# A fifth group of five turned by DMA ahead of the last rows, and x held until earlier transfers have landed

## The chip, the core and the metric

The kernel runs on one core of a Trainium2 chip. A core has TensorE (matmuls; PE in the profile, its weight loads PEld), VectorE (DVE), ScalarE (ACT), GpSimd (POOL) and SyncE (SP), each with its own instruction stream, and 16 DMA engines that all streams share. SP and GpSimd issue this kernel's transfers: SP's make up the queue "hardware_dynamic" of the profile, GpSimd's "software_dynamic". Matmuls write to PSUM banks; VectorE and ScalarE empty them to SBUF. The metric is the device time of one execution in microseconds (us), the median of several.

## What is computed

A mix along the sequence in the frequency domain, and then a mixer with a low-rank part and a hidden layer, for 8 batches of 3136 positions with 256 channels:

```python
X = np.fft.rfft(x, axis=1)                  # x: 8 x 3136 x 256
y = np.fft.irfft(X * F, n=3136, axis=1)     # F = filt_r + 1j * filt_i
h = y.transpose(0, 2, 1) @ U @ V            # rank 32
u = y + h.transpose(0, 2, 1)
out = u + np.maximum(u @ w_ch1, 0) @ w_ch2  # 256 -> 1024 -> 256
```

Inputs and output are float32; the matmuls take float16.

## The kernel before

**Stages of one batch.** The transform of length 3136 is split as 49 x 64. Stage 1 (`f1`) multiplies x by a matrix of the 49-point transform and stores the result in DRAM (`ct1`, `ct0`, L256 and L257). Batches 2 to 7 load it back turned as the tiles `a2`: four loads on SP, issued at once (L330 and L327, the first 512 KB ahead of a 32 KB and two more of 512 KB). Batches 0 and 1 turn it on TensorE instead. Stage 3 (`mid`) does the 64-point transform (`pz`, L385), the product with the filter on VectorE (`uv`, L393 to L398) and the way back (`pe`, L344), and stores its result in DRAM (`ct2`, L363) in three parts. `load_e2` loads the parts back as rows of the tile `eb` (L417), each in two halves; a part can be loaded when its last store has landed. `rank` computes the low-rank part and spreads it over 32 more rows of `eb` (L439). Stage 4 (`s4`, L457) multiplies `eb` by a constant matrix and gives u, transposed, in the tile `ut` (two buffers).

**Groups.** The mixer works through the 25088 positions in 49 groups of 512. Group n has eight steps `mm1` (L489, hidden layer, ReLU on ScalarE at L492), and, one group later, eight steps `mm2` (L522) that add into a PSUM bank `pc` (two banks). A slot is one step of both: slot 8n+t runs `mm1` of group n and `mm2` of group n-1. After steps 3 and 7 of `mm2` half a group is moved by VectorE from `pc` to `och` (two buffers, used in turn by the groups), and after step 7 GpSimd stores the group (L542).

**The u in `u + ...`.** The output is not transposed and `ut` is. Either TensorE adds u: eight matmuls with `ut` as weights and the identity as moving data (`residual`, L514), and VectorE copies the sum (L538). Or the group's stretch of `ut` is turned by two DMA transposes on SP (`turn_u`, L502, one for each half of the channels) into the tile `tur` (three buffers), and VectorE adds it while it empties `pc` (L535). 35 of the 49 groups are in the set `turning`. Of the six groups that begin in each batch's stretch, the first straddles two batches; for batches 2 to 6 of the loop, groups 10, 16, 22, 28 and 34 are the fifth, and are added by TensorE, like these first ones.

**What sets the order.** The program is scheduled by hand: each engine runs its instructions in the order in which the program issues them. The list `plan` has, for each of the 392 slots, generators that are advanced by a step after that slot's `mm1` and `mm2`. In the loop at L618, batch b's stages 3 and 4 lie in the slots from `a = S[b-1]` to `z = S[b]` (for b = 2: 48 to 96), in which the mixer works on the batch before; `e = z - 20` (22 from b = 6 on) is where stage 3 ends. The last part of the rows is loaded at `e + 1`, a2 of batch b+1 at `e + 2`, `s4` begins at `e + 8`. The four loads of x for batch b+1 are dealt to slots a-8, a-6, a-4 and a-2 (L640). GpSimd's stream from there on has only output stores and loads of x; those loads wait for stage 1 of the batch before, which is through by then.

Of the kernel before, what the change touches and what calls it, by code (L numbers as in the profile page):

```python
# [14 lines left out]
NB = 8  # L15
# [14 lines left out]
def row_of(k1, part):  # L30

    return 4 * (2 * ((k1 - 1) % 8) + part) + (k1 - 1) // 8
# [47 lines left out]
def kernel(  # L80
# [11 lines left out]
    nc = tc.nc  # L92
# [22 lines left out]
    def dram(t, off, dims):  # L115
        return bass.AP(tensor=t, offset=off, ap=[list(d) for d in dims])
# [7 lines left out]
    def load_x(b, c):  # L124
        t = sb.tile([98, 8 * DM], F16, tag="x", bufs=4, name="x")
        for a, n in ((0, 96), (96, 2)) if b == 0 else ((0, 98),):
            nc.gpsimd.dma_start(t[a:a + n], dram(x.tensor, (b * SEQ + 8 * c + 32 * a) * DM, [[32 * DM, n], [1, 8 * DM]]))
        xt[b, c] = t
# [68 lines left out]
    seen = cst.tile([128, 4], F16)  # L197
# [95 lines left out]
    def turn(b, g):  # L293
        if g == 3:
            t = a20[b]
            pt = bank("z" if b else "o", "pt", F16)
            for dh in range(2):
                nc.tensor.transpose(pt[0:64, 128 * dh:128 * dh + 128], t1[b][1][:, dh, :], idn)
            nc.scalar.copy(t[0:64], pt[0:64, 0:DM])
            return t  # L300
        t = sb.tile([128, 8, DM], F16, tag="a2", bufs=3, name="a2")
        for half in range(2):
            pt = bank("m" if b == 0 and g == 1 and half == 0 else "z", "pt", F16)
            if b == g == half == 0:
                unread(pt.bitcast(F32), 2)
            for i in range(4):
                for dh in range(2):
                    nc.tensor.transpose(pt[:, 256 * i + 128 * dh:256 * i + 128 * dh + 128],
                                        t1[b][0][:, dh, 8 * g + 4 * half + i, :], idn)
            (nc.scalar.copy if half or (g and b == 0) else nc.vector.tensor_copy)(  # L310
                t[:, 4 * half:4 * half + 4, :].rearrange("p k d -> p (k d)"), pt)
        return t
# [2 lines left out]
    PAIRS = [(k, k + 1) for k in range(1, NK, 2)]  # L315
    e3 = {}

    def mid(b, tag="z"):
        a2 = {}

        def load_a2(g):
            if b < 2:
                a2[g] = turn(b, g)
                return
            if g == 3:
                t = a20[b % 2]
                nc.sync.dma_start(t[0:64], ct0[b].ap())  # L327
            else:
                t = sb.tile([128, 8, DM], F16, tag="a2", bufs=3, name="a2")
                nc.sync.dma_start(t, dram(ct1[b], 8 * g * DM, [[24 * DM, 128], [1, 8 * DM]]))  # L330
            a2[g] = t

        def s3(ks, uv, o):
            n = len(ks) * DM
            i = (ks[0] - 1) // 2
            pe = bank(tag, "pe")

            direct = b == 0 and ks[0] > 22
            ms = (gmp, gsmp) if direct or not ks[0] else (gm, gsm)
            if b == 0 and ks[0] > 8:  # L340

                unread(pe, 1)
            for f, w in enumerate(ms if b == 0 else ms[:1]):
                nc.tensor.matmul(pe[:, 0:n], w, uv[:, f, o:o + n], start=(f == 0), stop=(b > 0 or f == 1))  # L344
            if not ks[0]:
                e3[b, 6] = sb.tile([128, DM], F16, tag="e30", bufs=1, name="e30")
                nc.scalar.copy(e3[b, 6], pe[:, 0:n])

                nc.sync.dma_start(eb[96:97, :, :], e3[b, 6][0:64])
                return  # L350
            if i % 2 == 0:
                e3[b, i // 2] = sb.tile([128, 4, DM], F16, tag="e3", bufs=6, name="e3")
            t = e3[b, i // 2]
            nc.scalar.copy(t[:, 2 * (i % 2):2 * (i % 2) + 2, :].rearrange("p k d -> p (k d)"), pe)  # L354
            if direct:
                for n, k in enumerate(ks):
                    for part in range(2):
                        (nc.sync if part else nc.gpsimd).dma_start(
                            eb[32 + row_of(k, part):33 + row_of(k, part), :, :],
                            t[64 * part:64 * part + 64, 2 * (i % 2) + n, :])  # L360
            elif i % 2 or b == 0 and i == 10:
                n = 4 if i % 2 else 2
                nc.sync.dma_start(dram(ct2[b][i // 4], 2 * (i % 4 // 2 * 2) * 128 * DM, [[DM, 128], [128 * DM, n], [1, DM]]), t[:, 0:n, :])  # L363

        if b == 0:
            spread_filters(0)
        for g in (0, 3, 1, 2) if b > 1 else (0, 3):
            load_a2(g)
        if b > 1:
            yield  # L370
        todo = []
        first_at = 2 if b < 2 else 6
        for i, ks in enumerate(PAIRS[:first_at] + [(0,)] + PAIRS[first_at:]):
            n = len(ks) * DM
            if b == 0 and i == 1:
                spread_filters(1)
            if b < 2 and i in (3, 7):
                load_a2(i // 4 + 1)
            pz = bank("z", "pz")
            if b == i == 0:  # L380
                unread(pz, 2)
            if ks[0]:
                src = a2[(ks[0] - 1) // 8]
                k = (ks[0] - 1) % 8
                nc.tensor.matmul(pz, a2m, src[:, k:k + 2, :].rearrange("p k d -> p (k d)"), start=True, stop=True)  # L385
            else:
                nc.tensor.matmul(pz[:, 0:n], a20m, a2[3], start=True, stop=True)
            o = 512 if ks[0] % 4 == 3 else 0
            if o == 0:
                uv = sb.tile([128, 2, 1024], F16, tag="uv", bufs=4, name="uv")  # L390
            zin = bass.AP(tensor=pz.tensor, offset=pz.offset, ap=[[pz.ap[0][0], 128], [0, 2], [1, n]])
            fin = view(fab[:, 0, ks[0], 0:1], 0, [[NK * DM, 2], [1, n]])
            nc.vector.tensor_mul(uv[:, :, o:o + n], zin, fin)  # L393
            todo.append((ks, uv, o))
            if b and (o or not ks[0]):

                nc.vector.tensor_sub(uv[0:64, 0, 0:o + n], uv[0:64, 0, 0:o + n], uv[64:128, 1, 0:o + n])  # L397
                nc.vector.tensor_add(uv[64:128, 0, 0:o + n], uv[64:128, 0, 0:o + n], uv[0:64, 1, 0:o + n])  # L398
            if len(todo) > (3 if b else 2):
                s3(*todo.pop(0))  # L400
            yield
        for n, it in enumerate(todo):
            s3(*it)
            if b or n == 0:
                yield
        if b == 0:
            load_e2(0, 2, [0])
            for part in range(3):
                load_e2(0, part, [1])
        yield  # L410
# [71 lines left out]
    def utv(b):  # L482
        return ut[b].rearrange("p h q r -> p h (q r)")
# [14 lines left out]
    def turn_u(gr):  # L498
        gr.tu = sb.tile([128, 2, 4, 128], F16, tag="tur", bufs=3, name="tur")
        for b, t0, o, n in gr.seg:  # L500
            for dh in range(2):
                nc.sync.dma_start(gr.tu[:, dh, :, :], utv(b)[:, dh, t0:t0 + n], transpose=True)  # L502
        yield

    def residual(gr, o, i):
# [42 lines left out]
    def deal(gen, count, a, z):  # L548
        for i in range(count):
            plan[max(0, int(a + i * (z - a) / count))].append(gen)  # L550

    def later_x(b, c):
        load_x(b, c)
        yield

    def turn_at(at, n):
        turning.add(n)
        plan[at].append(turns[n])
# [59 lines left out]
    for b in range(1, NB):  # L618
        a, z = S[b - 1], S[b]
        e = z - (17 if b == 1 else 20 if b < 6 else 22)  # L620
        deal(mids[b], 13, a + {1: 8, 2: -3}.get(b, -5), e - 4)
        deal(mids[b], 4, e - 4, e)
        for p, at in enumerate((e - 5, e - 4, e + 1)):
            plan[at].append(loads(b, p))
        deal(ranks[b], 6, e, e + 6)
        if b + 1 < NB:

            plan[z - 12 if b == 1 else e + 2].append(mids[b + 1])

        n = a // 8 + (1 if b > 1 else 2)  # L630
        for i in range(3):
            turn_at(a + (15 if b == 1 else 1) + i, n + i)
        turn_at(z - (15 if b == 1 else 9), z // 8 - 1)
        deal(s4s[b], 16, e + 8, z - 2)
        if b == 1:
            deal(f1s[1], 12, 1, 8)
        if b + 1 < NB:

            for c in range(4):
                plan[a + (9 if b == 1 else -8) + 2 * c].append(later_x(b + 1, c))  # L640
            deal(f1s[b + 1], 16, a + (21 if b == 1 else 10), z - (13 if b == 1 else 20))
# [43 lines left out]
```

## Time and profile before

| | before |
|---|---|
| median of 3 runs, us | 509.52 |
| the three runs, us | 506.11, 509.73, 509.52 |
| profiled execution, us | 511.49 |
| its span (first to last instruction), us | 509.7 |
| mean granted TensorE clock | 0.989 |
| residual matmuls (L514) | 120, busy 15.5 us |
| transposes (L502) | 70, 1.35 us median to issue one on SP |
| moved by SP's queue, by GpSimd's | 55.06 MB, 41.58 MB |

Durations come from the profiled execution. "Busy" of TensorE counts a matmul from its start to the modelled end of its pipeline, so that neighbours overlap; what a matmul costs is read from the starts. The granted clock is 1.00 or 0.50 of full speed, and the half-clock stretches before the end last 3.41 and 6.83 us. The page's 40 slices (12.7 us each) show where TensorE, its clock and the DMA engines fall off:

```profile
PE   4887899969999999999999999999999999999996
PEclk9998999998999999999999999999999999999999
DMA  8988769997568985899578995899688447443233
```

The costliest groups on TensorE, ScalarE and VectorE (busy us, mean ns of one, idle before it and what ended that):

```profile
L492 ACT ACTIVATE h<-phh 128x512 f16<-128x512 f32 x392 | 236.1, 605 | 87.4 <-PE phh L489 86.6
L522 PE MATMUL pc<-w2sb,h 128*128 128x256 f16 x1568 | 234.8, 273 | 1.3 <-DMA w2sb<-in_moe_w_ch_dram 0.8
L489 PE MATMUL phh<-ut,w1sb 128*128 128x512 f16 (+7 forms) x896 | 234.5, 354 | 0.4 <-DVE ut L464 0.4
...
L393 DVE TENSOR_TENSOR uv<-pz,fab 128x1024 f16<-128x1024 f32 (+1 forms) x104 | 120.6, 1178 | 15.0 <-PE pz L385 13.5
L535 DVE TENSOR_TENSOR och<-pc,tur 128x512 f32<-128x512 f32 (+1 forms) x71 | 48.4, 682 | 77.7 <-PE pc L522 76.5
```

### The profile page before, as it was taken

Reading aid. Unit: us, or ns where it says so; the run is one execution under the profiler, and the core shown is the slowest. Engines: PE = TensorE matmul, PEld = TensorE weight load, DVE = VectorE, ACT = ScalarE, POOL = GpSimd, SP = SyncE. Lnnn points to the kernel's source line nnn. Section 1 sums busy time; section 2 is a strip of 40 time slices with the busy share of each in tenths; the row PEclk is TensorE's granted clock in tenths of the full one; section 3 lists DMA queues with packets and bytes.
Section 4 is the critical chain, followed back from the end, with each engine's and each line's share of the span. In section 5 each row is a group of like instructions: output and inputs, shape, how many; then the busy total and the mean of one; then the engine's idle time right before and its main releaser. Section 6 shows DMA issues by size and latency. Waiting matters only on the chain.

```text
span 509.7 us, 11525 instructions
## 1 busy us (share of the span) xinstructions
PE 483.3 (95%) x4572; PEld 339.6 (67%) x4572; DVE 351.5 (69%) x470; ACT 375.3 (74%) x704; POOL 80.4 (16%) x123
## 2 busy tenths in 40 slices
PE   4887899969999999999999999999999999999996
PEld 4536566756666777677667777677677766776664
DVE  5887699457866898479757887579847896732122
ACT  6865779945896689867896689767996677666662
POOL 6662110020100200120101101021001010101110
PEclk9998999998999999999999999999999999999999
DMA  8988769997568985899578995899688447443233
GB/s 195 164 211 193 115 143 232 256 232 189 159 191 274 235 201 158 253 284 195 162 228 287 195 197 156 263 262 179 208 247 246 125 115 228 125 125 105 80 107 125
DMA packets 105471, 97.39 MB, mean 191 GB/s; under 512 B 42931, under 2 KB 89971, under 8 KB 105416
## 3 DMA queue, kind: packets, MB, share of 16 engines
q1 hardware_dynamic: 90712, 55.06, 43.3%
q0 software_dynamic: 14704, 41.58, 31.2%
q8 instruction: 36, 0.59, 0.5%
q14 instruction: 19, 0.16, 0.1%
HBM read 55.20 MB, written 47.78 MB: 202 GB/s over the span
## 4 chain that ended last, share of the span: by engine, by line
PE 79%; DMA 9%; DVE 5%; ACT 2%; issue 0%; POOL 0%; ACTq 0%; SPq 0%
PE pc L522 30%; PE phh L489 29%; PE pu L457 5%; PE pf L249 4%; PE pe L344 4%; PE pz L385 4%; DVE uv L393 3%; DMA ct<-e 3%; DMA eb<-ct 2%; DMA w2sb<-in_moe_w_ch_dram 2%; DMA a<-ct 2%; PE pc L514 1%; PE ph L424 1%; ACT e L354 1%; ACT h L492 1%; ACT asb L254 1%
## 5 line engine op out<-in xcount | busy, mean ns | idle before, releaser
L492 ACT ACTIVATE h<-phh 128x512 f16<-128x512 f32 x392 | 236.1, 605 | 87.4 <-PE phh L489 86.6
L522 PE MATMUL pc<-w2sb,h 128*128 128x256 f16 x1568 | 234.8, 273 | 1.3 <-DMA w2sb<-in_moe_w_ch_dram 0.8
L489 PE MATMUL phh<-ut,w1sb 128*128 128x512 f16 (+7 forms) x896 | 234.5, 354 | 0.4 <-DVE ut L464 0.4
L522 PEld LDWEIGHTS <-h 128*128 128x128 f16 x1568 | 151.9, 98 | 93.2 <-issue 3.1
L393 DVE TENSOR_TENSOR uv<-pz,fab 128x1024 f16<-128x1024 f32 (+1 forms) x104 | 120.6, 1178 | 15.0 <-PE pz L385 13.5
L535 DVE TENSOR_TENSOR och<-pc,tur 128x512 f32<-128x512 f32 (+1 forms) x71 | 48.4, 682 | 77.7 <-PE pc L522 76.5
L542 POOL DMA_DIRECT2D out_dram<-och x48 | 38.8, 809 | 392.8 <-DVE och L535 265.4
L489 PEld LDWEIGHTS <-w1sb 128*128 128x128 f16 x896 | 80.2, 98 | 21.0 <-issue 2.1
L354 ACT CAST e<-pe 128x512 f16<-128x512 f32 x96 | 56.6, 591 | 16.4 <-PE pe L344 15.5
L464 DVE CAST ut<-pu 128x392 f16<-128x392 f32 x92 | 48.8, 560 | 18.5 <-PE pu L457 16.9
L254 ACT CAST asb<-pf 98x512 f16<-98x512 f32 x96 | 57.2, 599 | 0.1
L439 DVE COPY eb<-h 32x4096 f16<-32x4096 f16 x32 | 38.2, 1231 | 13.8 <-ACT h L436 13.8
L457 PE MATMUL pu<-sv,eb 97*128 97x49 f16 x1024 | 40.5, 187 | 3.4 <-DMA eb<-ct 3.4
L344 PE MATMUL pe<-uv,m 128*128 128x512 f16 (+1 forms) x117 | 41.3, 371 | 2.5 <-DVE uv L393 2.4
L457 PEld LDWEIGHTS <-eb 97*128 97x128 f16 x1024 | 38.2, 98 | 5.6 <-DVE eb L439 2.8
L385 PE MATMUL pz<-a,m 128*128 128x512 f16 x96 | 36.7, 384 | 5.3 <-DMA a<-ct 4.3
L249 PE MATMUL pf<-x,ws 98*98 98x256 f16 x192 | 36.7, 273 | 0.1
L397 DVE TENSOR_TENSOR uv<-uv 64x1024 f16<-64x1024 f16 (+1 forms) x49 | 30.9, 630 | 1.7
L398 DVE TENSOR_TENSOR uv<-uv 64x1024 f16<-64x1024 f16 (+1 forms) x49 | 30.7, 627 | 0.7
L538 DVE COPY och<-pc 128x512 f32<-128x512 f32 x28 | 19.4, 691 | 15.1 <-PE pc L514 14.6
L249 PEld LDWEIGHTS <-ws 98*98 98x98 f16 x192 | 22.8, 125 | 9.5 <-issue 0.8
L462 ACT CAST ut<-pu 128x392 f16<-128x392 f32 x36 | 17.5, 485 | 8.1 <-POOL seen L605 4.0
(80 smaller groups left out, 235.7 us busy)
## 6 DMA issues: line engine op xcount, KB each, us to landing
out_dram<-och POOLq DMA_DIRECT2D x48, 512.0 KB, 4.5
ct<-e SPq DMA_DIRECT2D x47, 256.0 KB
eb<-ct SPq DMA_DIRECT2D x46, 256.0 KB
x<-in_x_dram POOLq DMA_DIRECT2D x28, 392.0 KB, 8.4
ct<-asb SPq DMA_DIRECT2D x24, 384.0 KB
a<-ct SPq DMA_DIRECT2D x18, 512.0 KB
x<-in_x_dram POOLq DMA_DIRECT2D x4, 384.0 KB, 8.0
tur<-ut SPq DMA_TRANSPOSE x70
```

The source lines that it names most:

```text
L249: nc.tensor.matmul(pf[0:98, 256 * s:256 * s + 256], ws[:, (8 * c + j) * 98:(8 * c + j + 1) * 98], t[:, j, :], start=(s == 0), stop=True, s ...
L254: nc.scalar.copy(dst, src)
L344: nc.tensor.matmul(pe[:, 0:n], w, uv[:, f, o:o + n], start=(f == 0), stop=(b > 0 or f == 1))
L354: nc.scalar.copy(t[:, 2 * (i % 2):2 * (i % 2) + 2, :].rearrange("p k d -> p (k d)"), pe)
L385: nc.tensor.matmul(pz, a2m, src[:, k:k + 2, :].rearrange("p k d -> p (k d)"), start=True, stop=True)
L393: nc.vector.tensor_mul(uv[:, :, o:o + n], zin, fin)
L457: nc.tensor.matmul(pu[:, NQ * i:NQ * i + NQ], eb[:, 8 * n + i, d], sv[:, 8 * g + i, :], start=(i == 0), stop=True, skip_group_check=True)
L464: nc.vector.tensor_copy(dst, src)
L489: nc.tensor.matmul(ph[:, o:o + n], w1sb[:, dh, 128 * t:128 * t + 128], utv(b)[:, dh, t0:t0 + n], start=(dh == 0), stop=(dh == 1), skip_gro ...
L492: nc.scalar.activation(h, ph, RELU)
L522: nc.tensor.matmul(o, gr.h[tt][:, 128 * i:128 * i + 128], w2sb[:, tt, :], start=(tt == 0), stop=(tt == 7 and gr.n in turning), skip_group_ ...
L535: nc.vector.tensor_add(dst.rearrange("p g (h d) -> p g h d", h=2), src.rearrange("p (g h d) -> p g h d", h=2, d=128), gr.tu[:, :, a:a + n, ...
```

## The change

1. For batches 2 to 6, the fifth group of the stretch (10, 16, 22, 28 and 34) joins the set `turning`. Its two transposes are issued in slot `e`: on SP after stage 3's last store and stage 1's last store of those slots, and ahead of the last part of the rows.
2. The third turned group of a stretch (9, 15, 21, 27, 33 and 39) is issued in slot a+8 in place of a+3. By then a buffer of `tur` is free.
3. `last_in[b]` holds a piece of the last tile that SP was told to fill for batch b: the last tile of a2 for batch 2, and the turned stretch of group 11, 17, 23 or 29 for batches 3 to 6. For batches 3 to 7 GpSimd copies four elements a partition of it into the tile `seen` before the first load of x. So GpSimd, whose stream is in order, issues x of batch 3 once a2 of batch 2 has landed, and x of batches 4 to 7 once that group's transposes have landed.

```diff
@@ mid(), load_a2
                 nc.sync.dma_start(t, dram(ct1[b], 8 * g * DM, [[24 * DM, 128], [1, 8 * DM]]))
+                if g == 2:
+                    last_in[b] = t[:, 7, 0:4]
@@ turn_u(gr)
                 nc.sync.dma_start(gr.tu[:, dh, :, :], utv(b)[:, dh, t0:t0 + n], transpose=True)
+        if gr.n % 6 == 5:
+            last_in[gr.n // 6 + 2] = gr.tu[:, 1, 3, 0:4]
@@ later_x(b, c)
+        if c == 0 and b > 2:
+            nc.gpsimd.tensor_copy(seen, last_in[b - 1])
         load_x(b, c)
@@ for b in range(1, NB)
         deal(ranks[b], 6, e, e + 6)
+        if 1 < b < NB - 1:
+            turn_at(e, z // 8 - 2)
...
         for i in range(3):
-            turn_at(a + (15 if b == 1 else 1) + i, n + i)
+            turn_at(a + (15 + i if b == 1 else (1, 2, 8)[i]), n + i)
```

More of the change, by code (lines that the diff above doesn't have):

```diff
@@ L316 @@
     e3 = {}
+    last_in = {}
     def mid(b, tag="z"):
```

## The prediction

> **What bounds the kernel.** I read the page first (busy shares, the chain that ended last), then the waits of TensorE alone, then the chain piece by piece around each of TensorE's waits. Batches count from 0; a slot is one pair of steps `mm1`/`mm2`, eight to a group, and slot 8n+t is step t of group n.
>
> ```profile
> PE 483.3 (95%) x4572; PEld 339.6 (67%) x4572; DVE 351.5 (69%) x470; ACT 375.3 (74%) x704; POOL 80.4 (16%) x123
> ...
> PE 79%; DMA 9%; DVE 5%; ACT 2%; issue 0%; POOL 0%; ACTq 0%; SPq 0%
> ```
>
> And TensorE's waits (us in total, times, longest):
>
> ```profile
> PE pz L385 <- DMA a<-ct: 4.3, 1, 4.3
> PE pu L457 <- DMA eb<-ct: 3.4, 3, 2.5
> ```
>
> TensorE is the bound: every instruction taken off it counts, and every wait put before it counts. After the first 60 us it has three waits worth a line: one of 4.27 us for a2 of batch 2, and 0.24 and 0.62 us (batches 2 and 5) of the 3.4 for the last rows of `eb`. The first, by the chain and by windows (columns: stretch, its length, busy time of PE, PEld, DVE, ACT, POOL, granted clock, DMA share, GB/s):
>
> ```profile
> 105.78 8.83 DMA a<-ct
> 114.61 0.05 issue
> 114.66 0.61 PE pz L385
> ```
>
> ```profile
> 110.40:114.60 4.20, 0.00 (x0) 0.00 (x0) 0.39 (x1) 0.48 (x1) 0.00 (x0) 0.74 1.25 271
> 114.70:119.20 4.50, 4.50 (x17) 2.25 (x18) 1.71 (x2) 1.19 (x2) 0.00 (x0) 0.50 0.99 266
> 119.30:124.00 4.70, 4.70 (x41) 3.27 (x40) 4.62 (x7) 2.96 (x6) 0.79 (x1) 1.00 1.10 252
> ```
>
> The reader is to see that TensorE does nothing for 4.2 us, and then runs at half clock until 119.27. What a2 competes with is in GpSimd's timeline: the four loads of x for batch 3 are issued just ahead of a2.
>
> ```profile
> 102.88 0.75 POOL L542 DMA_DIRECT2D out_dram<-och  x1 [8.17 <-DVE och L535]
> 103.62 2.18 POOL L127 DMA_DIRECT2D x<-in_x_dram  x4
> 119.70 0.79 POOL L542 DMA_DIRECT2D out_dram<-och  x1 [13.90 <-DVE och L535]
> ```
>
> Second, the chain into stage 4 of batch 2: the last store of stage 3, its landing, the last rows, TensorE. It is tight in every batch: s4 starts 0.05 to 0.25 us after these rows' first half has landed.
>
> ```profile
> 152.86 5.63 DMA ct<-e
> 158.49 0.02 issue
> 158.51 3.38 DMA eb<-ct
> 161.89 0.05 issue
> 161.94 0.59 PE pu L457 x16
> ```
>
> Landings of SP's transfers below are read from the trace's semaphore events (16 steps a transfer), those of GpSimd's from its issues.
>
> **Residual matmuls removed.** Groups 10, 16, 22, 28 and 34 lose 8 matmuls of L514 each, 40 in all. The row's 220 ns is the time through the pipeline; what a pair costs is where the next matmul starts:
>
> ```profile
> 167.96 0.28 PE L514 MATMUL pc<-idn,ut 128*128 128x128 f16 x2
> ...
> 168.07 0.58 PE L457 MATMUL pu<-sv,eb 97*128 97x49 f16 x16
> ```
>
> 0.11 us a pair, so 20 x 0.11 = **2.2 us less**, all on the path. VectorE's addition (L535, 682 ns) replaces a copy (L538, 691 ns): nothing.
>
> **x of batch 3 waits for a2 of batch 2.** This takes x off the DMA engines while a2 moves. Lost before: 4.27 us idle, and 114.66 to 119.27 at half clock, 2.3 us: 6.6 us. The first a2 load is issued at 105.78; a 512 KB transfer that runs alone (the output stores at 138.86 and 307.31) lands 3.2 to 3.3 us after its issue, so 109.1, and TensorE asks at 110.39. Against the store and rows beside it, batch 3's took 6.4 us: 112.2, a wait of 1.8 left. I take **6.6 us less** (4.8 to 6.6), by the lone row, since the store of 102.88 lands at 106.99.
>
> What is late next: on GpSimd, x and then group 4's output store queue behind the new wait. a2's last load (issued 108.31) lands near 112; x takes some 10 us of its queue (9 to 11.3 in batches 3 to 6) and lands at 123.5; the store behind it lands 2.9 to 4.8 us after x in those batches, with turned stretches between: 126.6. Its buffer is wanted by group 6's copy, which started at 132.25 and would start at 125.6. VectorE waits 1.0 us, and TensorE, which at 134.78 took a bank that VectorE had left at 134.21, some 0.5. I take **1.0 us more** (0 to 4, and 2.3 of half clock with the longest).
>
> **The fifth group turned ahead of the last rows.** Two transposes now stand on SP between stage 3's last stores and the rows, five times. SP itself has the room: it is free at 154.62 and waits until 158.49, and two issues take 2.5 to 3.2 us. The queue hasn't: the store of stage 1 (L256) issued at 153.55 lands at 159.51, and transposes behind another transfer have landed 1.0 us after it in pairs (102.42 to 103.47, 169.80 to 170.85, x's 181.80 to 182.79). So they land at 160.5, and in batches 3 to 6, where that store landed at 215.39, 271.87, 328.25 and 383.40, at 216.4, 272.9, 329.3 and 384.4. The rows' first half needs 1.9 to 2.8 us from first packet to landing: with 2.2 they land at 162.7, 218.6, 275.1, 331.5, 386.6, that is 0.8, 0.8, 1.2, 0.7 and 1.2 later than before; less 0.3 of slack, **4.4 us more**. Ends: 0, if rows queued early need no longer than the stores L363 that landed 0.6 and 0.8 us behind a turned stretch; 12.5, if a whole turned stretch (packets 100.4 to 103.0, 2.6 us) comes on top in each batch. I keep 4.4, since rows are reads and nothing shows them faster. Behind the rows a2 of the next batch moves by as much; it has landed 4.8 us before use in batch 3 (166.14 against 170.97).
>
> **The third turned stretch five slots later; x of batches 4 to 7.** Its two transposes go past one store of stage 3 on SP, and past nothing on GpSimd. SP no longer stands for a buffer (at 122.55 to 128.24) ahead of stage 3's stores; their rows are loaded from 148.50 on: nothing. Those x wait for a turned stretch that landed at 170.85 while the store ahead of x on its own queue landed at 172.13: x moves by about 1 us. Stage 1 reads it after 187 against a first landing of 175.20, and the store behind it has 1.7 to 4.1 us before its buffer is wanted: nothing (0 to 1).
>
> **A rule on the queues.** Transposes issued from 174.22 on landed from 182.17 on, after the last x (181.80), and SP's queue moved no packet from 171 to 181.8: I let them wait for x. The Trainium skill ("DMA: Bandwidth & Descriptors", Queues, rings and completion order) has each DMA engine alternate between queues packet by packet. By that rule the turned stretches would be through before x ends, group 4's store would land some 1.5 us sooner, the term of 1.0 would vanish and the sum would be 1.0 us lower; the trace disagrees.
>
> **Sum.** -2.2 - 6.6 + 1.0 + 4.4 = -3.4 us. The profiled execution took 511.49 us (span 509.7 and 1.8 around it): 508.1. The median of the runs is 2.0 us below that execution: **506.1 us**.
>
> **Rivals.**
> - *The rows are hidden.* Between 157 and 160 the DMA engines are 40% busy; if the transposes fit in there, the 4.4 falls away: -7.8, 501.7. For it: engines that finish the stores early are idle. Against: the three pairs above landed only after the last of the transfer ahead.
> - *The rows are late by a whole turned stretch* (slower). 2.6 us in each of five batches, +12.5 in place of 4.4: +4.7, 514.2. It decides from 1.6 us a batch ((2.2 + 6.6 - 1.0) / 5). Where TensorE stood 2.54 us before stage 4 of batch 0, 3.4 us at half clock followed, and at 110.39 the clock fell after 2.05 us; 1.7 us more in three batches gives 519.3. The Trainium skill ("TensorE: Matmul & The Clock Gate", Part 1) puts the fall at an idle window of about 3.4 us, which would leave it at 514.2; the trace shows it sooner.
> - *Batch 2's wait moves.* x and the store behind it keep VectorE, and then TensorE, for 4 us in slot 61 with 2.3 us of half clock: 6.3 of the 6.6 are given back, -2.2 - 0.3 + 4.4 = +1.9, 511.4. So too if a2 is late for another reason than x, and the change doesn't do what it says. Against it: by the DMA packets SP's queue moved almost nothing from 106 to 109, when a2 had been issued, while GpSimd's kept the engines 77 to 91% busy.
>
> **How the numbers follow.** Chances: forecast 0.40 (own range 503.5 to 509), rows hidden 0.25, rows late 0.20, wait moved 0.15. 1% is 5.1 us, about what a measurement can tell from no change: bounds 504.4 and 514.6. Faster: nearly all of the hidden rows and the forecast's lower end, 0.33; slower: rows late with a slower clock, and a little of the moved wait, 0.16; within, 0.51. The range from 501 to 515 leaves out the hidden rows with no new wait at all and the late rows at a slower clock.
>
> **What would show it.** TensorE's wait for a2 of batch 2 and the half clock from 112.4 on are gone; L514 has 80 instructions; x of batch 3 is issued after a2's last landing; VectorE waits for an output store near slot 59; s4 waits for `eb` in five batches by about 1 us. It is wrong if those waits are near zero or over 1.6 us each, or if a2 still comes late.

## The result, and the profile after

| | before | changed |
|---|---|---|
| median of 22 executions each, us | 510.24 | 511.58 |
| lowest and highest | 503.04, 514.16 | 507.27, 518.09 |
| mean of the 22 | 509.6 | 511.9 |
| profiled execution, its span, us | 511.49, 509.7 | 510.14, 508.3 |

The ratio is 1.009, with a 95% interval from 1.0061 to 1.012: the changed kernel is slower, by 2.3 us in the mean, where 3.4 us less were forecast. The ratios here leave out every execution more than 1.5% above the fastest of the same kernel, and for a kernel whose executions spread from 503 to 514 us that cuts into the ordinary spread, so differences between the means of all executions stand beside them.

The single profiled executions point the other way (510.14 against 511.49), and that is the first thing to read: one profile of a kernel with such a spread doesn't say which of two is faster. It does say where the time lies. The slices of the changed kernel, 12.7 us each:

```profile
PE   4786899999798999999999999999998999999997
PEclk9999999999999999999999999999999999999999
DMA  8997669979969994999979995999889346553253
```

The hole in slice 9 (before, TensorE at 6, and the clock at 8 in slice 10) has gone, and a 7 has come in slice 11, from 127 to 140 us. TensorE's and VectorE's waits (us in total, times, longest):

```profile
DVE och L545 <- DMA out_dram<-och: 5.2, 2, 4.1
PE pu L462 <- DMA eb<-ct: 5.2, 3, 3.0
PE pf L249 <- DVE uv L398: 3.2, 1, 3.2
```

The wait for a2 (4.3 us before) isn't in the list any more. In its place VectorE waits 4.1 us for an output store and TensorE 3.2 us for VectorE. The wait for rows of `eb` rose from 3.4 to 5.2 us, part of which was in batch 0 in both; two more waits before stage 4, 1.29 us in batch 2 and 0.70 in batch 4, are in the list under "issue". The stretches in which the prediction had read the hole of before (columns as there), in the changed kernel:

```profile
110.40:114.60 4.20, 4.20 (x47) 2.96 (x46) 3.49 (x5) 2.84 (x5) 0.19 (x1) 1.00 0.89 267
114.70:119.20 4.50, 4.50 (x40) 3.12 (x38) 4.42 (x6) 3.24 (x6) 2.97 (x5) 1.00 0.89 123
...
124.00:130.50 6.50, 5.42 (x39) 3.65 (x38) 2.41 (x5) 5.31 (x10) 0.00 (x0) 1.00 1.01 259
```

TensorE is busy without a break at full clock until 124, and the new hole follows. The chain of waits leads from a2 to it:

```profile
108.54 5.64 DMA a<-ct
...
114.31 0.02 POOL seen L562
...
114.86 0.53 POOL x L127
...
117.04 13.47 DMA out_dram<-och
...
130.60 0.69 DVE och L545
131.29 0.03 issue
131.32 1.24 DVE uv L398
132.56 0.04 issue
132.60 0.38 PE pf L249 x2
```

The reader is to see one string of events: a2's last load lands at 114.19, GpSimd's copy into `seen` follows, then the four issues of x, then group 4's store, which lands 13.47 us after its issue because x is ahead of it on its queue. VectorE's copy for group 6 needs that store's buffer; it had been ready at 126.50. The wait has been moved, not removed.

Second, the rows. SP's stream in slot `e` of batch 2 (start, length, what was issued):

```profile
151.47 0.71 SPq L257 DMA_DIRECT2D ct<-asb  x1
152.28 3.56 SPq L507 DMA_TRANSPOSE tur<-ut  x2
155.97 1.17 SPq L422 DMA_DIRECT2D eb<-ct  x2
```

By the semaphore events stage 1's store landed at 157.07, the two transposes at 157.62 and 158.06, and the first half of the rows at 160.28, which is 2.2 us after them; TensorE stood from 159.08 to 160.37.

### The profile page after: what moved, and what is told of

Same layout as the page of the kernel before. It is cut to its first block, busy times and chain, and to the rows that moved or that the text cites. A ratio compares the mean times of both kernels' runs of the same rounds, so it can differ in the third digit from the quotient of the medians.

```text
span 508.3 us, 11480 instructions
## 1 busy us (share of the span) xinstructions
PE 477.2 (94%) x4532; PEld 334.8 (66%) x4532; DVE 350.0 (69%) x470; ACT 375.8 (74%) x704; POOL 81.7 (16%) x128
## 4 chain that ended last, share of the span: by engine, by line
PE 76%; DMA 12%; DVE 5%; ACT 2%; issue 2%; POOL 1%; SPq 1%; DVEq 0%; POOLq 0%; ACTq 0%
PE pc L529 30%; PE phh L494 29%; PE pu L462 5%; PE pf L249 4%; PE pe L349 4%; PE pz L390 3%; DVE uv L398 3%; DMA out_dram<-och 3%; DMA eb<-ct 2%; DMA w2sb<-in_moe_w_ch_dram 2%; DMA x<-in_x_dram 2%; POOL x L127 1%; DMA a<-ct 1%; PE ph L429 1%; DMA fab<-in_filt_i_dram 1%
## 5 line engine op out<-in xcount | busy, mean ns | idle before, releaser
L542 DVE TENSOR_TENSOR och<-pc,tur 128x512 f32<-128x512 f32 (+1 forms) x81 | 55.3, 683 | 79.5 <-PE pc L529 78.2
L359 ACT CAST e<-pe 128x512 f16<-128x512 f32 x96 | 56.6, 591 | 15.7 <-PE pe L349 14.3
L444 DVE COPY eb<-h 32x4096 f16<-32x4096 f16 x32 | 38.2, 1231 | 13.8 <-ACT h L441 13.8
L462 PE MATMUL pu<-sv,eb 97*128 97x49 f16 x1024 | 39.2, 185 | 8.0 <-DMA eb<-ct 5.2
L545 DVE COPY och<-pc 128x512 f32<-128x512 f32 x18 | 12.4, 690 | 16.3 <-PE pc L521 9.1
```

Source lines behind the costliest of these rows:

```text
L462: nc.tensor.matmul(pu[:, NQ * i:NQ * i + NQ], eb[:, 8 * n + i, d], sv[:, 8 * g + i, :], start=(i == 0), stop=True, skip_group_check=True)
L542: nc.vector.tensor_add(dst.rearrange("p g (h d) -> p g h d", h=2), src.rearrange("p (g h d) -> p g h d", h=2, d=128), gr.tu[:, :, a:a + n, ...
```

## Where the time went, slot by slot

To add up what moved, the start of each slot (its first `mm1`) was read from seven profiles: four of the kernel before and three of the changed one (all but the first of each come from the experiments below). The stretches of the table hold all of it up to the start of the last slot. A stretch "at rest" is the shortest one that any profile shows.

| stretch, us | before, four profiles | changed, three profiles | mean |
|---|---|---|---|
| start to slot 44 | 107.67, 107.30, 107.09, 107.85 | 108.39, 108.24, 106.31 | +0.2 |
| slots 44 to 48 (a2; at rest 4.73) | 11.24, 10.80, 8.83, 8.35 | 4.73, 4.73, 4.73 | -5.1 |
| slots 48 to 76 (at rest 33.55) | 33.73, 33.67, 33.55, 33.55 | 36.89, 35.68, 37.92 | +3.2 |
| five times 12 slots from `e` on (rows; at rest 64.85) | 66.14, 66.96, 66.78, 65.64 | 69.99, 69.67, 73.89 | +4.8 |
| all other slots after 76 | 282.26, 282.26, 282.26, 282.25 | 280.03, 280.33, 280.03 | -2.1 |
| sum | | | +1.0 |

The row of all other slots is the cleanest: the four profiles of before agree within 0.01 us there. The sum is 1.0 us slower by seven profiles, 2.3 by 44 executions; with a spread of some 2 us from profile to profile these agree.

## The experiments

Each kernel was run beside the kernel before on the same chip. "Mean" is the difference between the means of all executions of a run and those of the kernel before beside it.

| kernel | median (executions) | before beside it | ratio, 95% interval | mean |
|---|---|---|---|---|
| before, again | 511.68 (6) | 509.75 (29) | 1.0108, 1.0054 to 1.0161 | +2.4 |
| waits only | 510.07 (12) | 509.75 | 1.0044, 0.9997 to 1.0092 | -0.1 |
| fifth only | 514.51 (12) | 509.75 | 1.0064, 1.0014 to 1.0115 | +5.2 |
| fifth behind the rows | 510.19 (12) | 509.75 | 1.006, 1.0015 to 1.0105 | +0.3 |
| x of batch 3 behind the store | 507.68 (11) | 510.02 (27) | 0.9983, 0.9936 to 1.003 | -0.7 |
| change, x of batch 3 behind the store | 512.76 (11) | 510.02 | 1.0026, 0.9984 to 1.0067 | +3.2 |
| both orders, no waits | 530.11 (5) | 510.02 | | +19.1 |
| all later x behind the store, no waits | 513.04 (11) | 510.02 | 1.0021, 0.9974 to 1.0068 | +4.6 |
| change, batch 2's turned groups late | 515.65 (11) | 511.16 (21) | 1.0084, 1.0039 to 1.0128 | +4.8 |
| turned groups clear of x and rows | 509.57 (11) | 511.16 | 0.9971, 0.9939 to 1.0003 | -0.5 |
| change, again | 511.52 (12) | 509.83 (16) | 1.0043, 1.0007 to 1.0079 | +2.0 |
| change, wait for batch 3 alone | 515.93 (5) | 509.83 | 1.0118, 1.0062 to 1.0173 | +5.5 |

### How much one profile of the kernel before says

The kernel before ran again, once with its times and twice for a profile; the changed kernel likewise once each. Neither kernel is altered.

> The kernel before, once more, for the spread of its own executions. Theory 1 (every execution before has the wait for a2 of batch 2 that its profile showed, 4.27 us and 2.3 us at half clock): the executions lie within about 1 us of each other apart from disturbed ones, with a mean granted clock near 0.989. Theory 2 (that wait is there in some executions only, as x and a2 happen to meet): two groups some 6 us apart, about 504 to 507 with a clock near 0.995 and 510 to 513 with a clock near 0.989, and a profile of this run may lack the wait.

> The kernel before, a second profile more. Theory 1: TensorE waits 4.3 us for a2 of batch 2 as in the two profiles so far. Theory 2: that wait is missing or short in about 3 of 10 executions, and those take some 6 us less (503 to 507); such a profile would show it.

> The kernel before, a third profile more. Theory 1: 4.3 us of wait for a2 of batch 2 again. Theory 2: the wait is missing or short in about 3 of 10 executions, which take some 6 us less.

The six executions of the first gave a ratio of 1.0108 against the very same kernel. So an interval of such a ratio is too narrow by itself to call half a per cent, and small differences below are read from all executions and from the profiles' stretches together. The last of the profiles has for a2 of batch 2 (the waits of TensorE):

```profile
PE pz L385 <- DMA a<-ct: 1.8, 1, 1.8
```

Over the four profiles this wait was 4.3, 4.3, 2.4 and 1.8 us, and what slots 44 to 48 took beyond 4.73 was 6.5, 6.1, 4.1 and 3.6 us; the executions took 511.49, 511.42, 508.87 and 508.03 us. The prediction had the costliest of the four before it.

> After itself once more, in one session with before. From the profiles by stretches (slot 44 to 48; 48 to 76; five times 12 slots from e on): four profiles of before have 6.5, 6.1, 4.1 and 3.6 us of a2's wait (5.1 in the mean), kernels with the wait of x 2.4 to 5.5 us near slot 61, the fifth group ahead of the rows 5.1 to 8.5 us against before's 0.8 to 2.1. Theory C (the sum of these means, -5.1 + 3.9 + 5.3 - 2.0): about 2 us slower than before over all executions. Theory of the prediction: 3 us faster. The profile of this run: 4.73 us from slot 44 to 48, 36 to 39 from 48 to 76, rows 5 to 8 us over 12.97 each.

> After, a third profile. Theory C: 4.73 us from slot 44 to 48, 36 to 39 us from 48 to 76, the five stretches from e on 5 to 8 us over 5 x 12.97. Were the first profile's rows (5.1) and its 3.3 us near slot 61 typical, those again.

The changed kernel's second timing, with the profile's execution 13 in all, was 2.1 us above the kernel before beside it, like the first. Its profiles show VectorE's wait in slot 61 each time (4.1, 2.9 and 3.5 us), and a slower late part in the last (rows 2.56 us late in batch 5 and 2.38 in batch 6, the latter with 3.41 us at half clock behind it).

### One part at a time

Waits only: the kernel before with part 3 of the change alone.

```diff
-        if 1 < b < NB - 1:
-            turn_at(e, z // 8 - 2)
...
-            turn_at(a + (15 + i if b == 1 else (1, 2, 8)[i]), n + i)
+            turn_at(a + (15 if b == 1 else 1) + i, n + i)
```

> The kernel before with the waits of x alone: no fifth group is turned and the third turned group stays in slot a+3. Theory 1: -6.6 us for a2 and about +3.3 us for VectorE's wait for group 4's store (as in the profile of after), so 3 us faster than before. Theory 2: 3 us faster than the slower executions of before and 3 us slower than the faster ones, so between -1 and +2 us on the median, with a narrower spread than before. In both, TensorE waits about 3 us near slot 61 and not for a2.

a2's wait is gone and the new one is there without the fifth group (waits of VectorE and TensorE):

```profile
DVE och L545 <- DMA out_dram<-och: 5.1, 2, 4.6
...
PE pf L249 <- DVE uv L398: 3.7, 1, 3.7
```

Slots 44 to 48 took 4.73 us, and slots 48 to 76 took 39.07, that is 5.5 over rest with 3.41 us at half clock. Holding x until a2 has landed gained nothing by itself in these 12 executions: -0.1 us in the mean.

Fifth only: the change without any wait of GpSimd ahead of x.

```diff
     def later_x(b, c):
-        if c == 0 and b > 2:
-            nc.gpsimd.tensor_copy(seen, last_in[b - 1])
         load_x(b, c)
```

> After without any wait of x: the fifth groups turned ahead of the rows and the third one moved. Theory 1 and 2: -2.2 us for the 40 matmuls and about +3.8 us for the rows (the steps of the profile of after: 1.0, 0.7, 0.9, -0.5, 1.8), so 1.5 us slower than before; the wait for a2 is as before, none at slot 61. Theory 3 (the rows are most of the loss, and the profile of after was a lucky one): 4 us or more slower, with a lower clock.

Slots 48 to 76 are at rest (33.55), which ties the new wait to part 3 from the other side. a2's wait is back (2.51 us), and stage 4 starts 1.42, 0.63, 0.76 and 1.82 us late in batches 2, 4, 5 and 6. The rows' stretches hold 5.4 us over rest and all other slots 280.03, as in the changed kernel. Against the means of the kernel before, these are 3.9 us more, 2.2 less and, for a2, 1.0 less: 0.7 us slower. All executions say 5.2, with a standard deviation of 4.3. Its one profile, of an execution at 512.08 us, doesn't show the rest.

Fifth behind the rows: the change with the fifth group's transposes one slot later, behind the rows' issue on SP.

```diff
-            turn_at(e, z // 8 - 2)
+            turn_at(e + 1, z // 8 - 2)
```

> After with the fifth group's transposes issued one slot later, behind the last rows on SP instead of ahead of them; the waits of x stay. Theory 1: the 3.8 us of the rows are gone, 5 us faster than before and 3.8 us faster than after. Theory 2: 3.8 us faster than after too, so about 2.5 us faster than before on the median. If the rows were not the cost, it equals after.

SP's stream of batch 2 has the two in the other order:

```profile
156.55 1.16 SPq L422 DMA_DIRECT2D eb<-ct  x2
157.76 2.99 SPq L507 DMA_TRANSPOSE tur<-ut  x2
```

The rows' stretches fall from 5.1, 4.8 and 9.0 us over rest to 0.9, and stage 4 waits in batch 2 alone (0.64 us). So the place ahead of the rows is what those waits come from. But the transposes now meet x and the stores behind it:

```profile
DVE och L545 <- DMA out_dram<-och: 13.8, 4, 4.5
```

That is four times in place of two, and the other slots take 4.2 us more than the changed kernel's. What the rows gain is mostly given back: 0.3 us above the kernel before, 1.9 below the changed one.

### What holds the store in slot 61

Three theories stood: x itself is long; the turned groups of batch 2, in flight beside x, make it long; or it is only the order, x ahead of the store on GpSimd. Two kernels change the order of x and the store, by dealing x of batch 3 to slots 48 to 54 (behind group 4's store) in place of waiting for a2; the second of them keeps the waits for later batches (`b > 3`).

```diff
-                plan[a + (9 if b == 1 else -8) + 2 * c].append(later_x(b + 1, c))
+                plan[a + (9 if b == 1 else 0 if b == 2 else -8) + 2 * c].append(later_x(b + 1, c))
```

> The kernel before with the four loads of x for batch 3 dealt to slots 48, 50, 52 and 54 instead of 40 to 46, so that GpSimd issues them behind group 4's store and after a2; no wait, no fifth group. Theory A (the gain of a2 was given back because that store stood behind x): TensorE waits neither for a2 nor near slot 61, -6.5 us against an execution of before that has the a2 wait, so a median near 504 to 505 where before has 510. Theory B (a2 is late by itself, or x late in its turn stops stage 1): a wait of 2 us or more for a2 or for x near slot 58 stays, and the median is 508 or more.

> After with batch 3's wait of x replaced by the same order of issue (x behind group 4's store); the fifth group stays ahead of the rows and the waits of batches 4 to 7 stay. Theory A: the 3.3 us near slot 61 and the half clock after it are gone, 3 to 5 us faster than after; rows late by some 4 us in all as in after. Theory B: no different from after.

With the store ahead of x no output store is waited for near slot 61 in either. In the first, done to the kernel before, TensorE then waits for x itself, in stage 1:

```profile
PE pu L457 <- DMA eb<-ct: 5.2, 2, 2.8
...
PE pf L249 <- DMA x<-in_x_dram: 3.2, 1, 3.2
```

Slots 48 to 76 take 38.56 us, so x arrives too late for its reader where it arrived too early for the store. This profile is of the slowest of the eleven executions, though (514.6 us; the median is 507.68), so how often x is late by that much isn't shown. In the second, slots 48 to 76 are at rest (33.55), but stage 4 of batch 2 starts 2.07 us late and 3.41 us of half clock follow, and its rows' stretches hold 8.5 us over rest. That order, too, brings no gain that these executions show.

In the third kernel batch 2's turned groups are issued at slots 59, 60 and 62, when x has mostly landed.

```diff
-            turn_at(a + (15 + i if b == 1 else (1, 2, 8)[i]), n + i)
+            turn_at(a + (15 + i if b == 1 else (11, 12, 14)[i] if b == 2 else (1, 2, 8)[i]), n + i)
```

> After with the three turned groups of batch 2 issued in slots 59, 60 and 62 instead of 49, 50 and 56, once x of batch 3 has landed. Theory A (x and group 4's store are late because a turned stretch is in flight beside them: in the profile of after the DMA engines move 140 to 180 GB/s from 118 to 126 us, where they are over 90% busy): x and the store land by 127, VectorE's wait for the store falls from 4.1 us to under 1.5 and TensorE's from 3.2 to under 1; about 3 us faster than after. Theory B (x alone takes that long): VectorE still waits 3 us or more.

The executions are no faster, and in the profile VectorE still waits 3.20 us, from 124.94 on; the chain:

```profile
113.25 0.53 POOL x L127
...
115.43 12.62 DMA out_dram<-och
128.04 0.03 issue
128.07 0.02 DVEq L545
128.09 0.04 issue
128.14 0.69 DVE och L545
```

x takes 13.4 us from its first issue to its last landing (126.63) without a turned stretch beside it for its first 10 us, and 14.2 to 15.2 us in the three profiles of the changed kernel. So x does most of it, and the turned groups seem to add one to two microseconds; they don't each time, for with the fifth group behind the rows they stood in their old slots and x took 12.7 us.

That is not a slowness of batch 3. In the last kernel of the next section, where x is issued into an empty queue in every batch, it took 12.4 us in batch 2's stretch and 12.9, 12.3, 14.0 and 12.5 us in those after it, counted in the same way. The 9 to 11.3 us of the prediction are times on the queue: in the profile before, x of the next stretch was issued at 167.53, the store ahead of it landed at 172.13, and x's last load at 181.80, which is 9.7 us after that store and 14.3 after the issue.

### Versions meant to be better

Both orders, no waits: x of batch 3 behind the store, the fifth group behind the rows, no copies into `seen`. The next has x of all later batches behind the store (`0` in place of `-8` for every `b > 1`).

```diff
-        if c == 0 and b > 2:
-            nc.gpsimd.tensor_copy(seen, last_in[b - 1])
...
-            turn_at(e, z // 8 - 2)
+            turn_at(e + 1, z // 8 - 2)
...
-                plan[a + (9 if b == 1 else -8) + 2 * c].append(later_x(b + 1, c))
+                plan[a + (9 if b == 1 else 0 if b == 2 else -8) + 2 * c].append(later_x(b + 1, c))
```

> x of batch 3 behind group 4's store, the fifth groups turned one slot later, behind the rows, the third one moved as in after, and no wait of x at all. Theory A with the terms as measured: -2.2 us for the matmuls, -6.5 for a2 where before has that wait, +0.4 for the rows: a median near 502 to 503. If x of batches 4 to 7 without a wait runs into the turned stretches, VectorE waits for a store in some batches, 1 us each, and it is near 505.

> The same with x of every later batch dealt to slots a to a+6, behind the output store: no store stands behind x, so no wait of VectorE for a store in any batch; if x is late instead, TensorE waits for x at stage 1 (slot a+10 on). Theory A: equal to combo or 1 to 2 us faster. Else slower by the waits for x.

The first was the slowest of all. Its chain in batch 5:

```profile
334.61 0.83 SPq L507
335.44 0.04 issue
335.49 26.41 DMA tur<-ut
...
362.02 0.69 DVE och L542
362.71 1.14 DVE uv L398
363.85 0.04 issue
363.90 0.59 PE pe L349
```

A transpose, which lands 6.1 us after its issue in the median of the changed kernel's page, took 26.41 us. x was issued 1.14 us behind it (336.63) and landed at 362.13. In between, the engines look busy and move almost nothing (columns as above):

```profile
344.00:348.00 4.00, 4.00 (x36) 3.17 (x35) 3.92 (x6) 2.82 (x5) 0.79 (x1) 1.00 1.33 31
348.00:352.00 4.00, 4.00 (x36) 3.12 (x34) 1.99 (x3) 3.02 (x7) 0.00 (x0) 1.00 0.79 88
```

TensorE stood 10.75 us and then ran 10.24 us at half clock. The second has no such collision in its profile, and why not isn't shown; TensorE waits for x in stage 1 instead, four times for 6.4 us, and it is 4.6 us slower than the kernel before.

Turned groups clear of x and rows: the change with the fifth group behind the rows, and the other three of a stretch issued in later slots, where x has mostly landed.

```diff
-            turn_at(e, z // 8 - 2)
+            turn_at(e + 1, z // 8 - 2)
...
-            turn_at(a + (15 + i if b == 1 else (1, 2, 8)[i]), n + i)
+            turn_at(a + (15 + i if b == 1 else (11, 12, 14)[i] if b == 2 else (8, 9, 11)[i]), n + i)
```

> The waits of x as in after, the fifth groups behind the rows, and in every batch the other three turned groups issued only after x has landed (slots a+11, a+12, a+14 in batch 2, a+8, a+9, a+11 later). Theory A: a2's 6.5 us and the matmuls' 2.2 us are kept, rows cost 0.4, no wait for a store in any batch: near 502 to 503 on the median, 7 us below before's executions with the a2 wait. Theory B: no better than after with the fifth behind the rows, 510.

It has the lowest ratio, 0.9971, and doesn't beat the kernel before by its interval; the mean is 0.5 us lower. Its profile, a good one at 506.67 us, has 33.74 us for slots 48 to 76 and rows 0.9 over rest; its other slots take 2.5 us more than the changed kernel's, most of it a store wait in batch 5. Slot 61 owes something to chance: in this execution TensorE had stood 4.89 us before stage 4 of batch 0, so it was further behind SP than elsewhere (a2 was issued 3.8 us ahead of slot 44, in the three profiles of the changed kernel 2.0 to 2.8), and the store that landed at 128.86 was wanted at 128.01.

### Whether the later waits for x do anything

```diff
-        if c == 0 and b > 2:
+        if c == 0 and b == 3:
```

> After with the wait of x in batch 3 alone; x of batches 4 to 7 waits for nothing. If those waits cost and bring nothing (the prediction), it equals after. If they keep a turned stretch from being in flight beside x (as in combo, where one then took 26 us to land and TensorE stood 10.75 us), it is slower than after, by 2 us or more on the median and with longer outliers; VectorE then waits for a turned stretch or a store in a later batch.

Without the waits of batches 4 to 7 the changed kernel is 3.4 us slower (means of 5 and 13 executions, 515.2 and 511.8). They were forecast to do nothing. The fifth group alone, without any of the waits, was slow in the same way; but six executions of the unaltered kernel were 2.4 us off, so 3.4 on five is not far above chance. In the one profile the rows' stretches hold 9.0 us over rest, within what the changed kernel's show (4.8 to 9.0), so which transfers the waits keep apart isn't shown.

## Why the prediction was wrong

Step by step, with what it took and what was measured:

| step | predicted | measured |
|---|---|---|
| 40 residual matmuls less | -2.2 | -2.1 |
| a2 of batch 2 | -6.6 | -5.1 (-3.6 to -6.5) |
| store behind x, slot 61 | +1.0 | +3.2 (+2.1 to +4.4) |
| rows behind the transposes | +4.4 | +4.8 (+3.3 to +7.5) |
| third turned later, x of batches 4 to 7 | 0 | 0 in the sum; the waits are perhaps worth 3 beside the fifth group |
| sum | -3.4 | +1.0 by profiles, +2.3 by executions |

**Residual matmuls: right.** The line of L521 in the changed kernel (duration ns min/median/max, first and last start):

```profile
L521 PE MATMUL pc<-idn,ut x80: 218/220/244, 61.9 to 466.0; 128*128 128x128 f16 x64, 128*64 128x128 f16 x16
```

There are 80 in place of 120, and nothing else moves the other slots: 0.11 us a pair was the price, read from where the next matmul starts and not from the 220 ns.

**Rows: right in mechanism, and in size in the mean.** In batch 2 the transposes landed 0.5 and 1.0 us after the store ahead, the rows 2.2 us after them, as worked out. That the mean of three profiles comes so near is in part luck, as they lie between 3.3 and 7.5. Neither the rival that the rows are hidden nor the one of a whole turned stretch in each batch holds, though the slowest profile has 2.56 and 2.38 us in two batches. The kernel with the fifth group behind the rows shows the cause. What the prediction lacked is that the other place isn't free either: behind the rows the same transposes make four store waits of 13.8 us in place of two of 5.2.

**a2: a failing step, of baseline.** "I take 6.6 us less ... by the lone row" counted the wait of one profile in full. That execution had the largest of four, and its 511.49 us lay above the median. The prediction then took another 2.0 us off the sum, "The median of the runs is 2.0 us below that execution". That removes part of the same excess twice: what makes that execution slower than the median is in part the very wait that was already taken off. The mean gain is 5.1.

**The store behind x: the failing step, and the largest miss.** "I take 1.0 us more (0 to 4 ...)" was put together from a2 landing "near 112", x landing at 123.5 and the store at 126.6. In the profile after they were at 114.19, 130.06 and 130.51. a2's last load took 5.6 us, beside the other three, against the 3.7 allowed; x landed 15.9 us after a2, 15.2 from its own first issue, against the 11.5 allowed; the store landed right behind x, 0.45 us, and not 3. The row taken for x, "9 to 11.3 in batches 3 to 6", counted loads that had stood on the queue behind a store. Behind the new wait the queue is empty when x is issued, and there, in the kernel with the turned groups clear of x and rows, x took 12.3 to 12.9 us in four of five stretches and 14.0 in the other. The rival "Batch 2's wait moves" described this exactly, with its place and its engine; it was given a chance of 0.15 and a price of 6.3, where 3.2 of 5.1 was given back. That its time of 511.4 us is so near the measured 511.58 is luck: its two sizes, 6.6 and 6.3, were measured as 5.1 and 3.2.

Neither miss turns the sign alone. With 3.2 for the store the sum is -1.2, with 5.1 for a2 as well it is +0.3.

**A rule on the queues: the outcome held, the reading didn't.** A transpose issued at 115.42 in the changed kernel landed at 130.29, just after x's last at 130.06. But SP's queue isn't still in between. From 120 to 127 us the queues of the changed kernel (packets, MB, share of 16 engines):

```profile
q0 software_dynamic: 340, 1.11, 99.5%
q1 hardware_dynamic: 309, 0.08, 8.6%
```

SP's queue moved nearly as many packets as GpSimd's and a fourteenth of its bytes: most of SP's are of 256 bytes, and most of GpSimd's of 4096. The Trainium skill ("DMA: Bandwidth & Descriptors", Queues, rings and completion order) lets each engine alternate between the queues packet by packet; counted in packets, this stretch of the trace agrees. The profile before is alike: from 171 to 181.8 SP's queue moved 833 packets, 159 of them between 172 and 180, so "no packet" was a misreading. Ten more transposes added 5440 packets under 512 bytes to the page, 544 each, and x's four loads have some 400 large ones: by turns of one packet a pair of transposes need not be through before x. So the 1.0 us that the prediction set beside the rule doesn't follow from it. The holding isn't strict either: with the fifth group behind the rows, the same transpose landed at 122.8 and x's last at 127.9.

With every size as measured, -5.1 + 3.2 + 4.8 - 2.1 is +0.8; the start, up to slot 44, makes it +1.0. The forecast's two ends for a2 and the store (4.8 and 4) would have given +1.4. Both were on the page, and the favourable one was taken in each.

**What stays open.** The executions say some 1 us more than the profiles' stretches, which is within their spread. Whether the later waits for x are really worth 3 us, and why, and when a turned group beside x makes it longer, wasn't settled.

## What to carry to other kernels

A wait put ahead of a load on an in-order queue moves everything behind it: follow the next store on that queue to whoever needs its buffer, and price it with the load's time from its issue on a queue as empty as it will be there, not with the time that is left of a load that has stood behind another. Before a wait's full length is counted as a gain, look at how it varies between executions, and never take the excess of a slow execution off twice. If the places for an added transfer all collide with something (here rows ahead, x behind), the gain must be larger than the cheapest collision: here 2.1 us of matmuls bought at least as much waiting on the queues.

## What the runs showed of the hardware

**A transpose in flight beside the loads of x is slow.** The loads of x turn float32 into float16 on the way and are issued by GpSimd. In the changed kernel's profile the longest transposes took 14.9, 13.7, 13.4, 13.2 and 13.0 us from issue to landing, all issued while x was in flight, against the page's median of 6.1; the packet counts above show SP's queue with as many packets as x's and far fewer bytes. Once it was much worse: a transpose issued 1.14 us ahead of x landed after 26.41 us and x after 25.5, and for 8 us the DMA engines were 79 to 133% busy by the profile and moved 31 to 88 GB/s, against 259 GB/s from 124 to 130.5 us in the changed kernel. That this one comes from the two kinds of transfer meeting is read from when they were in flight; it wasn't measured by itself.

**The clock looks at fixed windows of 3.41 us.** In each profile with more than one half-clock stretch, their starts lie multiples of 3.413 us apart. Laying that grid over TensorE's starts and modelled ends in 17 profiles, in windows that begin at full clock between 60 and 500 us, every window with 2.04 us or more of idle time was followed by half clock (14 of 14), of those with 1.71 to 2.02 us 3 of 9, and none with less. So it is not the length of a wait alone that decides, but how it falls on the grid: the 3.2 us in the changed kernel's profile were split into 1.71 and 1.47 and cost no clock, and 1.78 us of the kernel before, all in one window, cost 3.41 us at half clock. The Trainium skill ("TensorE: Matmul & The Clock Gate", Part 1) gives a free-running window of 3413 ns, and these runs agree; it speaks of an idle window, and here about 60% of one was enough.

**A single core's executions spread by 2%** (503.0 to 514.2 us, standard deviation 3.1 in 22) with the same program, and the wait for a2 alone was between 1.8 and 4.3 us in four profiles.
